# A router run once more on fewer tiles, logits in four column tiles, and loads on other queues and buffers

## The chip, the cores and the metric

The kernel runs on one core of one Trainium2 chip. The metric is the device time of one execution in microseconds (us), lower is better; several runs are made and the median counts. One further execution was recorded by the hardware profiler, and every row below is from that one. The engines are TensorE (PE, with its weight loads PEld), VectorE (DVE), ScalarE (ACT), GpSimd (POOL) and SyncE (SP), which here only issues DMAs. "L319" is line 319 of the kernel; the changed kernel's lines lie a few higher.

## The reference, cut to what matters

Three layers one behind the other, on 4 batches of 576 tokens of width 512 (8 heads of 64):

```python
def _attn_ref(q, k, v, phi):
    a = softmax of phi over the tokens
    k_m = np.einsum('bhsm,bhsd->bhmd', a, k)
    v_m = np.einsum('bhsm,bhsd->bhmd', a, v)
    scores = scale * np.matmul(q, k_m.transpose(0, 1, 3, 2))
    attn = softmax of scores over the 32 memories
    return np.matmul(attn, v_m).astype(np.float32)

def _moe_ref(x, w_in, w_out):
    h = x @ w_in
    g = h * (1.0 / (1.0 + np.exp(-h)))
    return (g @ w_out).astype(np.float32)

def _moe2_ref(x, w_gate, w_noise, noise, w1, w2):
    logits = x @ w_gate
    noise_scale = np.log1p(np.exp(x @ w_noise))
    noisy_logits = logits + noise_scale * noise
    top2 = np.argpartition(-noisy_logits, 2, axis=1)[:, :2]
    ...
    for e in range(E):
        for k in range(2):
            mask = top2[:, k] == e
            ...
            h = np.maximum(x[mask] @ w1[e], 0.0)
            out[mask] += top2_w[mask, k, None] * (h @ w2[e])
```

w_in (512 x 2048) and w_out (2048 x 512) arrive as float64; the 8 experts have w1 of 512 x 1024 and w2 of 1024 x 512.

## The kernel before, in words

**Attention and MLP.** The 2304 tokens are 18 tiles of 128: four whole ones in each batch, and a fifth that two batches share. Tiles 0 to 8 are those of batches 0 and 1, 9 to 12 of batch 2, 13 to 17 of batch 3 and the second shared one. The attention of a batch is folded into the first MLP matrix: `project` multiplies `w_in` by the batch's memories (L146), so that TensorE then goes from attention weights to the hidden layer (`mlp_h`, L258) and on to the output (`accumulate`, L280 to L282). Every operand is split into a high and a low part and takes three matmuls. ScalarE evacuates the hidden layer from PSUM with a tanh (L261), VectorE finishes the SiLU (L263), both make the two parts (L266, L267).

**Weights at the start.** `stage` brings a float64 block as pairs of 32-bit words into one of four buffers (tag `st`); `narrow` turns it into float32: ScalarE scales the upper word (L197), takes its sign (L198) and the lower word (L200, tile `lw`, one buffer), VectorE merges (L201), GpSimd multiplies by the sign (L202). There are 32 such steps. `w_in`, once narrowed, is also stored in DRAM (L220) and fetched again for each later batch into `wi`, two buffers (L214).

**The router.** When a tile of the MLP is done, `tile_a` copies it out (`xs`, L298) and stores it, `tile_b` transposes it (L312, L314: `xt`), `tile_c` computes 16 logits a token with four matmuls that accumulate in PSUM (L319), ScalarE copies them to `lz` (L320). `gate(j0, j1)` then works on tiles j0 to j1: some 30 small VectorE operations, a matmul for each token's rank in its expert (L396, L397), the slot (L414), and for each tile two indirect scatters of GpSimd into the table `tab_d` (L418). All scatters of a gate stand one behind the other in GpSimd's queue. Gates cover tiles 0 to 8, 9 to 12, 13 to 16 and 17.

**The experts.** `table(0)` loads the first expert's first rows of the table (L507, on SP's queue) and clips the index (L508); `gather(0)` fetches those tokens (L515), `flip` transposes them (L534). `fetch_w1(0, c)` and `split_w1(0, c)` load and split the first expert's w1 in four parts (L475; L483 on ScalarE, L484 on VectorE), in the `st` buffers. The experts follow in the tail (L551, L566, L571), writing to the output by scatter-add (L574).

**What sets the order.** The MLP runs in steps `s`, 32 for each batch (`SB`), its second half three steps (`LAG`) behind the first. Other work is hung on a step by `at(s, function, ...)`; the gates are called between two steps. The Tile framework then orders each engine's queue by priorities and adds the semaphores. Each engine runs its queue in that order, so one waiting instruction holds what stands behind it. PSUM has two `aux` and two `h` buffers for all short-lived products.

Of the kernel before, what the change touches and what calls it, by code (L numbers as in the profile page):

```python
# [20 lines left out]
NF = FF // 128  # L21
# [21 lines left out]
def body(ctx, tc, a):  # L43
# [21 lines left out]
    wgn = const.tile([128, 4, 16], F32, name="wgn")  # L65
# [127 lines left out]
    def narrow(t, m):  # L193
        top = t[:, :, 1].bitcast(F32)
        g = ap_.tile([128, 512], BF16, name="cg", bufs=2)
        mi = m.bitcast(I32)
        act.activation(m, top, AF.Copy, scale=2.0 ** -112)  # L197
        act.activation(g, top, AF.Sign)  # L198
        low = ap_.tile([128, 512], I32, name="lw", bufs=1)
        act.activation(low, t[:, :, 0].bitcast(U32), AF.Identity, scale=LOW, bias=lowb)  # L200
# [8 lines left out]
    def fetch_win(i):  # L209
        if i < NP:  # L210
            ST["i", i] = [stage(win[:, 2 * g:2 * g + 2, 2 * i * PW:2 * (i + 1) * PW]) for g in range(2)]
        else:
            WI[i] = m1.tile([128, 4, PW], F32, name="wi", bufs=2)
            sp.dma_start(WI[i].rearrange("p r f -> p (r f)"), win_d[i % NP])  # L214

    def narrow_win(i):
        WI[i] = m1.tile([128, 4, PW], F32, name="wi", bufs=2)
# [76 lines left out]
    XS, XT = {}, {}  # L294
# [21 lines left out]
    def tile_c(j):  # L316
        p = psum("aux", 2)
        for d in range(4):
            pe.matmul(p[:, :16], XT[j][:, d, :], wgn[:, d, :], start=(d == 0), stop=(d == 3))  # L319
        act.activation(lz[:, j, :], p[:, :16], AF.Copy)  # L320
# [7 lines left out]
    def routing_setup():  # L328
# [7 lines left out]
        for b in range(1, B, 2):  # L336
            j = TILES.index((b, 4))
            for x in range(2):
                pool.iota(tok[x * 64:(x + 1) * 64, j:j + 1], pattern=[[0, 1]], base=(b + x) * S - 64,
                          channel_multiplier=1, allow_small_or_imprecise_dtypes=True)  # L340
        sp.dma_start(wgn[:, :, 0:8], a["moe2_w_gate"].rearrange("(c p) e -> p c e", p=128))
# [129 lines left out]
    def fetch_w1(e, c):  # L471
        W1S[e, c] = P2["b"].tile([128, FE], F32, name="w1s", bufs=2) if e else \
            m1.tile([128, FE], F32, name="w1s", tag="st", bufs=4)
# [27 lines left out]
    def table(k):  # L501
# [5 lines left out]
        sp.dma_start(TAB[k].rearrange("p j w -> p (j w)"), t.rearrange("(p j) w -> p (j w)", j=n))  # L507
# [177 lines left out]
    ready = phi_max(0, 1)  # L685
    memory(0, 0)
    memory(0, 1)
    memory_t(0)
# [5 lines left out]
    with tc.issue_after(ready.ins):  # L694
        narrow_win(0)
# [47 lines left out]
    for b in range(B - 1):  # L743
# [10 lines left out]
        for k in range(1, n):  # L754
            at(s + k, tile_c, j + k)
            if k + 1 < n:
                at(s + k, tile_b, j + k + 1)
    s = 3 * SB
    at(s, open_a)
    at(s + 2, clear)  # L760
    for j in range(EARLY):
        at(s + 24 + 2 * j, flip, 0, j)
    for c in range(4):
        at(s + 4 + 4 * c, fetch_w1, 0, c)
        at(s + 10 + 4 * c, split_w1, 0, c)
# [13 lines left out]
    while s < total + LAG + 6:  # L779
# [4 lines left out]
        if s in (2 * SB, 4 * SB):  # L784
# [12 lines left out]
            else:  # L797
# [4 lines left out]
                for i, j in enumerate(range(13, 17)):  # L802
                    mlp_rest(b, range(cut[i], cut[i + 1]))
                    if j < 16:
                        tile_b(j + 1)
                    tile_c(j)
                gate(13, 17)
                mlp_rest(b, range(8, NF))
                for fn in (tile_a, tile_b, tile_c):
# [3 lines left out]
        if s == 2 * SB + LAG + 8:  # L813
            gate(0, 9)
# [44 lines left out]
```

## Time and profile before

| | us |
|---|---|
| median of 3 runs | 912.18 (911.67 to 913.01) |
| the profiled execution, its own time | 918.92 |
| its span in the trace | 917.1 |
| TensorE busy | 856.0 (93%) |
| VectorE busy | 462.0 (50%) |
| ScalarE busy | 366.3 (40%) |
| GpSimd busy | 252.2 (27%) |

The span is what the rows' times count from; 1.8 us of the execution lie around it. "Idle before" in a row is how long the engine stood still ahead of that instruction, and the name behind the arrow is what ended it ("issue": nothing that the profile shows; "remote": a semaphore whose setter it did not find). The granted clock is TensorE's, as a share of full speed.

### The profile page before, as it was taken

The page shows a single profiled execution, that of the slowest core. Times are in us where ns is not written, and L with a number is a line of the kernel's source. Part 1 is how long each engine was busy: PE and PEld are TensorE (multiplying, and loading weights), DVE is VectorE, ACT ScalarE, POOL GpSimd, SP SyncE. Part 2 cuts the span into 40 slices and gives each one's busy share as a digit, 9 for nine tenths or more (in the row PEclk, how much of TensorE's full clock was granted, in tenths as well). Part 3 has the DMA queues.
Part 4 walks back from the last instruction along what each step waited for, and adds up shares of the span by engine and source line. Part 5 has one row for each costly group of instructions (what it writes and reads, how often), then busy time and mean ns, then how long its engine had stood idle before and what let it go on. Part 6 is the DMA issues. An engine that isn't in the chain of part 4 may idle for free.

```text
span 917.1 us, 14389 instructions
## 1 busy us (share of the span) xinstructions
PE 856.0 (93%) x5504; PEld 724.5 (79%) x5504; DVE 462.0 (50%) x1070; ACT 366.3 (40%) x850; POOL 252.2 (27%) x279
## 2 busy tenths in 40 slices
PE   4698999999997899989999999999999999999995
PEld 2366678888885688868879998989989798897983
DVE  3787985575282755644553534344343444443410
ACT  3689974444232454443222532233323233231300
POOL 2555550000007000310342414234252352422311
PEclk9999999999999899999999999999999999999998
DMA  9798942532201118121243834364343644434311
GB/s 304 221 356 266 303 163 92 164 127 72 78 1 47 47 70 322 47 81 47 81 123 107 272 92 141 119 189 126 126 124 129 183 133 145 124 98 145 84 27 38
DMA packets 76166, 124.14 MB, mean 135 GB/s; under 512 B 27827, under 2 KB 39475, under 8 KB 76087
## 3 DMA queue, kind: packets, MB, share of 16 engines
q1 hardware_dynamic: 46343, 90.66, 30.0%
q0 software_dynamic: 29744, 32.46, 12.5%
q8 instruction: 45, 0.74, 0.3%
q14 instruction: 34, 0.28, 0.1%
HBM read 99.69 MB, written 23.81 MB: 135 GB/s over the span
## 4 chain that ended last, share of the span: by engine, by line
PE 71%; DVE 8%; ACT 6%; DMA 5%; issue 4%; POOL 3%; another core or an unknown queue 1%; SPq 1%; POOLq 0%; ACTq 0%; DVEq 0%
PE x L566 22%; PE x L551 11%; PE h L551 11%; PE h L258 7%; PE x L280 5%; PE x L282 4%; PE x L281 4%; PE aux L146 2%; PE aux L319 2%; PE aux L534 2%; DMA w1s<-moe_w 2%; POOL wo L202 1%; DMA kv<-kv 1%; DVE gl L267 1%
## 5 line engine op out<-in xcount | busy, mean ns | idle before, releaser
L566 PE MATMUL x<-w,gh 128*128 128x512 f32 (+5 forms) x640 | 202.4, 397 | 0.1
L566 PEld LDWEIGHTS x<-w,gh 128*128 128x128 f32 (+5 forms) x640 | 114.3, 183 | 28.0 <-ACT gh L553 0.5
L566 PE MATMUL x<-w,gl 128*128 128x512 f32 (+5 forms) x320 | 125.9, 393 | 0.2 <-DVE gl L554 0.2
L258 PE MATMUL h<-ah,wph 128*128 128x256 f32 (+1 forms) x512 | 113.3, 305 | 12.6 <-DVE th L263 4.8
L551 PE MATMUL h<-xh,w 128*128 128x290 f32 (+7 forms) x512 | 118.9, 303 | 0.0
L551 PE MATMUL x<-xh,w 128*128 128x290 f32 (+7 forms) x512 | 118.4, 303 | 0.0
L258 PEld LDWEIGHTS h<-ah,wph 128*128 128x128 f32 x512 | 90.6, 193 | 29.3 <-DVE th L263 8.1
L280 PE MATMUL x<-woh,gh 128*128 128x512 f32 x256 | 106.1, 417 | 4.5 <-ACT gh L266 2.2
L281 PE MATMUL x<-wol,gh 128*128 128x512 f32 x256 | 103.1, 403 | 6.4 <-issue 2.9
L282 PE MATMUL x<-woh,gl 128*128 128x512 f32 x256 | 102.0, 399 | 1.5 <-issue 1.0
L418 POOL DMA_INDIRECT tab_d<-rows,slot x36 | 35.4, 984 | 233.2 <-DVE slot L414 221.7
L263 DVE SCALAR_TENSOR_TENSOR th<-th,h 128x256 f32<-128x256 f32 (+1 forms) x128 | 57.7, 450 | 69.5 <-ACT th L261 53.5
L261 ACT ACTIVATE th<-h 128x256 f32<-128x256 f32 (+1 forms) x128 | 52.1, 407 | 90.7 <-PE h L258 72.0
L551 PEld LDWEIGHTS h<-xh,w 128*128 128x128 f32 x512 | 87.4, 189 | 0.3
L551 PEld LDWEIGHTS x<-xh,w 128*128 128x128 f32 x512 | 87.3, 188 | 0.0
L515 POOL DMA_INDIRECT xg<-x_d,gid x37 | 46.4, 1255 | 146.2 <-issue 76.9
L571 DVE SCALAR_TENSOR_TENSOR y<-x,tab,ex 116x512 f32<-116x512 f32 (+5 forms) x35 | 26.3, 750 | 108.0 <-PE x L566 103.6
L551 PE MATMUL x<-xl,w 128*128 128x290 f32 (+7 forms) x256 | 77.6, 303 | 0.5 <-DVE xl L538 0.5
L551 PE MATMUL h<-xl,w 128*128 128x290 f32 (+7 forms) x256 | 77.6, 303 | 0.0
L258 PE MATMUL h<-ah,wpl 128*128 128x320 f32 (+1 forms) x256 | 77.2, 302 | 0.3 <-DVE wpl L234 0.3
L574 POOL DMA_INDIRECT out<-y,tab x40 | 51.7, 1292 | 89.9 <-DVE y L571 82.8
L266 ACT ACTIVATE gh<-th 128x256 fp32r<-128x256 f32 x128 | 53.2, 416 | 52.9 <-DVE th L263 50.4
(158 smaller groups left out, 1421.7 us busy)
## 6 DMA issues: line engine op xcount, KB each, us to landing
w1s<-moe_w SPq DMA_DIRECT2D x32, 512.0 KB
w2s<-moe_w SPq DMA_DIRECT2D x32, 512.0 KB
wi<-win_d SPq DMA_DIRECT2D x24, 512.0 KB
kv<-kv SPq DMA_DIRECT2D x16, 650.0 KB
st<-moe_w_in SPq DMA_DIRECT2D x16, 512.0 KB
st<-moe_w_out SPq DMA_DIRECT2D x16, 512.0 KB
q<-qt SPq DMA_DIRECT2D x16, 288.0 KB
out<-z SPq DMA_DIRECT2D x1, 4608.0 KB
```

The source lines that it names most:

```text
L258: pe.matmul(p[:, :w], wt[:, g, c:c + 128], AH[b, g][at][:, t0:t0 + w], start=(n == 0), stop=(n == 5))
L261: act.activation(th[:, :w], p[:, :w], AF.Tanh, scale=0.5)
L263: dve.scalar_tensor_tensor(u[:, :w], th[:, :w], 1.0, p[:, :w], op0=OP.add, op1=OP.mult)
L266: act.activation(gh, u[:, :256], AF.Copy)
L280: pe.matmul(X2[j], gh[:, r], woh[f], start=(f == 0), stop=False)
L281: pe.matmul(X2[j], gh[:, r], wol[f], start=False, stop=False)
L282: pe.matmul(X2[j], gl[:, r], woh[f], start=False, stop=(f == NF - 1))
L418: st = pool.indirect_dma_start(out=tab_d, out_offset=bass.IndirectOffsetOnAxis(ap=slot[:, j, k:k + 1], axis=0), in_=rows.bitcast(I32)[:, j ...
L515: pool.indirect_dma_start(out=XG[k, j], out_offset=None, in_=x2_d if k else x2_d[:KNOWN, :], in_offset=bass.IndirectOffsetOnAxis(ap=GID[k] ...
L551: pe.matmul(p[:, :w], wt[:, d, c], x[:, d, r], start=(n == 0), stop=(n == 11))
L566: mm = pe.matmul(p, g[:, r], w[:, f, :], start=(n == 0), stop=(n == 23))
L574: st = pool.indirect_dma_start(out=a["out"], out_offset=bass.IndirectOffsetOnAxis(ap=TAB[k][:, j, 0:1], axis=0), in_=y, in_offset=None, bo ...
```

## The change

1. `gate(0, 9)` becomes `gate(0, 4)`, a batch earlier, and `gate(4, 9)` in the old place.
2. `tile_c` takes the padded gate weights `wgn` (four blocks of 128 x 32) as the stationary operand and the transposed tile as the moving one, so that the four matmuls write four blocks of 32 PSUM partitions. ScalarE copies 128 x 128 to `lt` (tag `st`). A new `tile_d`, a step later, transposes that on TensorE and adds the four blocks on VectorE.
3. `table(0)` is issued on GpSimd's queue.
4. Parts 2 and 3 of the first expert's w1 use the `wi` buffers, fetched at steps 20 and 21 and split at 24 and 27 of the last batch (before: 12 and 16, 18 and 22, in `st`); the flips go one step later.
5. `narrow_win(0)` is written ahead of batch 0's softmax, without its condition; `narrow` does the lower word first.

```diff
-    wgn = const.tile([128, 4, 16], F32, name="wgn")
+    wgn = const.tile([128, 4, 32], F32, name="wgn")
...
         mi = m.bitcast(I32)
+        low = ap_.tile([128, 512], I32, name="lw", bufs=1)
+        act.activation(low, t[:, :, 0].bitcast(U32), AF.Identity, scale=LOW, bias=lowb)
         act.activation(m, top, AF.Copy, scale=2.0 ** -112)
         act.activation(g, top, AF.Sign)
-        low = ap_.tile([128, 512], I32, name="lw", bufs=1)
-        act.activation(low, t[:, :, 0].bitcast(U32), AF.Identity, scale=LOW, bias=lowb)
...
         for d in range(4):
-            pe.matmul(p[:, :16], XT[j][:, d, :], wgn[:, d, :], start=(d == 0), stop=(d == 3))
-        act.activation(lz[:, j, :], p[:, :16], AF.Copy)
+            pe.matmul(p[d * 32:(d + 1) * 32, :128], wgn[:, d, :], XT[j][:, d, :], start=True, stop=True)
+        LT[j] = m1.tile([128, 128], F32, name="lt", tag="st", bufs=4)
+        act.activation(LT[j], p[:, :128], AF.Copy)
+
+    def tile_d(j):
+        p = spare(j)
+        pe.transpose(p[:, :128], LT.pop(j), ident)
+        dve.tensor_reduce(lz[:, j, :], p[:, :128].rearrange("p (d e) -> p e d", d=4)[:, :16, :], axis=AX.X, op=OP.add)
...
+        pool.memset(wgn, 0.0)
...
-            m1.tile([128, FE], F32, name="w1s", tag="st", bufs=4)
+            m1.tile([128, FE], F32, name="w1s", tag="st", bufs=4) if c < 2 else \
+            m1.tile([128, FE], F32, name="w1s", tag="wi", bufs=2)
...
-        sp.dma_start(TAB[k].rearrange("p j w -> p (j w)"), t.rearrange("(p j) w -> p (j w)", j=n))
+        (sp if k else pool).dma_start(TAB[k].rearrange("p j w -> p (j w)"), t.rearrange("(p j) w -> p (j w)", j=n))
...
     memory(0, 1)
+    narrow_win(0)
     memory_t(0)
...
-    with tc.issue_after(ready.ins):
-        narrow_win(0)
...
         for k in range(1, n):
+            at(s + k, tile_d, j + k - 1)
             at(s + k, tile_c, j + k)
...
-        at(s + 24 + 2 * j, flip, 0, j)
-    for c in range(4):
-        at(s + 4 + 4 * c, fetch_w1, 0, c)
-        at(s + 10 + 4 * c, split_w1, 0, c)
+        at(s + 25 + 2 * j, flip, 0, j)
+    for c, (x, y) in enumerate(((4, 10), (8, 14), (20, 24), (21, 27))):
+        at(s + x, fetch_w1, 0, c)
+        at(s + y, split_w1, 0, c)
...
+                mlp_rest(b, range(8, 10))
+                tile_d(16)
                 gate(13, 17)
-                mlp_rest(b, range(8, NF))
-                for fn in (tile_a, tile_b, tile_c):
+                mlp_rest(b, range(10, NF))
+                for fn in (tile_a, tile_b, tile_c, tile_d):
                     fn(17)
...
-        if s == 2 * SB + LAG + 8:
-            gate(0, 9)
+        if s == SB + LAG + 8:
+            gate(0, 4)
+        elif s == 2 * SB + LAG + 8:
+            gate(4, 9)
```

SP's queue around the first expert's weights `w1s`, before. `wi<-win_d` brings back narrowed weights, `x_d<-xs` stores finished tiles, `tab` is the table.

```order
L475 DMA w1s<-moe_w 128x1024
L214 DMA wi<-win_d 128x1024 x2
L475 DMA w1s<-moe_w 128x1024
L214 DMA wi<-win_d 128x1024 x2
L507 DMA tab_4275<-tab_d 128x6
L475 DMA w1s<-moe_w 128x1024 x2
L301 DMA x_d<-xs 128x512 x4
```

The same place in the changed kernel, and GpSimd's queue behind the scatters of gate(9,13) there.

```order
L483 DMA w1s<-moe_w 128x1024
L214 DMA wi<-win_d 128x1024 x2
L483 DMA w1s<-moe_w 128x1024
L214 DMA wi<-win_d 128x1024 x2
L483 DMA w1s<-moe_w 128x1024 x2
L301 DMA x_d<-xs 128x512 x4
```

```order
L363 MEMSET z 128x512
L425 DMA tab_d<-rows,slot 20480x2 x8
L515 DMA tab_4378<-tab_d 128x6
L516 TENSOR_SCALAR gid_4379<-tab_4378 128x3
L523 DMA xa<-x_d,gid_4379 128x512 x3
```

The table's load has left SP, where it stood ahead of the last two w1s, and stands on GpSimd between the scatters and the index step, where nothing stood.

ScalarE's first instructions, before and changed. `kvt` is batch 0's memories, `src` what it is made from; in the changed kernel the lower word is L198, the scaled upper word L199, the sign L200.

```order
L131 ACTIVATE src<-aux,rs 128x2x64
L197 ACTIVATE wi<-st 128x512
L131 ACTIVATE src<-aux,rs 128x2x64
L198 ACTIVATE cg<-st 128x512
L140 ACTIVATE kvt<-aux 128x256
L200 ACTIVATE lw<-st,lowb 128x512
L197 ACTIVATE wi<-st 128x512
L198 ACTIVATE cg<-st 128x512
L200 ACTIVATE lw<-st,lowb 128x512
L197 ACTIVATE wo<-st 128x512
```

```order
L131 ACTIVATE src<-aux,rs 128x2x64
L198 ACTIVATE lw<-st,lowb 128x512
L131 ACTIVATE src<-aux,rs 128x2x64
L199 ACTIVATE wi<-st 128x512
L200 ACTIVATE cg<-st 128x512
L199 ACTIVATE wi<-st 128x512
L198 ACTIVATE lw<-st,lowb 128x512
L200 ACTIVATE cg<-st 128x512
L140 ACTIVATE kvt<-aux 128x256
L198 ACTIVATE lw<-st,lowb 128x512
L199 ACTIVATE wo<-st 128x512
```

The evacuation of `kvt` stands behind five instructions of narrow steps instead of two, and `lw` ahead of its step's other two.

TensorE where batch 0's second tile gets its logits, before and changed.

```order
L280 MATMUL x_1752<-woh_90,gh 128x512
L281 MATMUL x_1752<-wol_106,gh 128x512
L282 MATMUL x_1752<-woh_90,gl 128x512
L258 MATMUL h<-ah_1408,wph 128x320
L319 MATMUL aux<-wgn,xt 128x16 x4
L258 MATMUL h<-ah_1409,wph 128x320
L258 MATMUL h<-ah_1408,wpl 128x320
L312 MATMUL aux<-ident,xs 128x128 x4
L258 MATMUL h<-ah_1488,wph 128x320
L258 MATMUL h<-ah_1489,wph 128x320
L258 MATMUL h<-ah_1488,wpl 128x320
L280 MATMUL x_1788<-woh_90,gh 128x512
```

```order
L258 MATMUL h<-ah_1409,wph 128x320
L325 MATMUL aux<-ident,lt 128x128
L258 MATMUL h<-ah_1410,wph 128x320
L258 MATMUL h<-ah_1409,wpl 128x320
L258 MATMUL h<-ah_1489,wph 128x320
L258 MATMUL h<-ah_1490,wph 128x320
L319 MATMUL aux<-xt,wgn 32x128 x4
L312 MATMUL aux<-ident,xs 128x128 x4
L258 MATMUL h<-ah_1489,wpl 128x320
L325 MATMUL aux<-ident,lt 128x128
L280 MATMUL x_1790<-woh_90,gh 128x512
L281 MATMUL x_1790<-wol_106,gh 128x512
```

The logits' four matmuls have 128 columns in place of 16, with operands exchanged, and a transpose of `lt` follows some instructions later for each tile.

## Rows read from the trace of the kernel before

**Rows 1.** Page, part 1: busy us, share and instructions of each engine, whole span.

```profile
PE 856.0 (93%) x5504; PEld 724.5 (79%) x5504; DVE 462.0 (50%) x1070; ACT 366.3 (40%) x850; POOL 252.2 (27%) x279
```

**Rows 2.** Windows: length, busy us (PE, PEld, DVE, ACT, POOL), granted clock, DMA share, GB/s.

```profile
60.00:120.00 60.00, 51.98 (x392) 36.94 (x392) 50.36 (x95) 54.07 (x120) 32.69 (x30) 1.00 0.86 287
283.50:303.00 19.50, 9.75 (x63) 6.36 (x63) 2.38 (x7) 1.80 (x5) 12.55 (x13) 0.80 0.02 1
303.00:306.00 3.00, 3.00 (x13) 2.64 (x12) 2.96 (x6) 0.62 (x2) 0.00 (x0) 0.61 0.00 0
344.00:361.50 17.50, 17.50 (x137) 14.85 (x136) 7.83 (x18) 6.56 (x20) 0.00 (x0) 1.00 0.98 352
377.30:387.20 9.90, 9.90 (x58) 8.78 (x57) 3.96 (x10) 3.38 (x10) 7.72 (x8) 1.00 0.34 108
396.50:408.00 11.50, 7.32 (x31) 5.62 (x31) 7.21 (x16) 5.87 (x16) 2.37 (x3) 0.85 0.36 116
```

**Rows 3.** Timeline of TensorE: start, us, line, names, count, idle before and its end.

```profile
288.93 1.10 PE L146 MATMUL aux<-q,kvt 64*32 64x320 f32 x16 [2.50 <-issue]
```

**Rows 4.** Timeline of GpSimd: scatters of gate(0,9), first, last; of gate(9,13), first.

```profile
276.82 1.13 POOL L418 DMA_INDIRECT tab_d<-rows,slot  x1 [138.76 <-DVE slot L414]
...
298.80 0.96 POOL L418 DMA_INDIRECT tab_d<-rows,slot  x1 [0.30 <-issue]
...
377.29 0.97 POOL L418 DMA_INDIRECT tab_d<-rows,slot  x1 [33.55 <-DVE slot L414]
```

**Rows 5.** Timeline of ScalarE: first MLP evacuation at the end of each.

```profile
299.16 0.39 ACT L261 ACTIVATE th<-h 128x256 f32<-128x256 f32 x1 [13.97 <-remote]
...
387.38 0.44 ACT L261 ACTIVATE th<-h 128x320 f32<-128x320 f32 x1 [3.05 <-PE h L258]
```

**Rows 6.** Timeline of SP's DMA queue: table and w1s.

```profile
391.73 0.33 SPq L507 DMA_DIRECT2D tab<-tab_d  x1
392.23 6.12 SPq L475 DMA_DIRECT2D w1s<-moe_w  x2
```

**Rows 7.** Timeline of ScalarE: splits of w1s.

```profile
396.04 1.15 ACT L483 ACTIVATE w<-w1s 128x512 fp32r<-128x512 f32 x2 [4.38 <-DMA w1s<-moe_w]
...
402.72 1.15 ACT L483 ACTIVATE w<-w1s 128x512 fp32r<-128x512 f32 x2 [2.63 <-DMA w1s<-moe_w]
```

**Rows 8.** Timeline of TensorE, 396 to 409 us: two gaps, the first flip.

```profile
398.39 0.51 PE L258 MATMUL h<-ah,wph 128*128 128x256 f32 x2 [1.86 <-DVE th L263]
...
404.23 0.70 PE L280 MATMUL x<-woh,gh 128*128 128x512 f32 x1 [2.04 <-ACT gh L266]
...
408.03 0.60 PE L534 MATMUL aux<-ident,xa 128*128 128x128 f32 x4
```

**Rows 9.** Timeline of TensorE: a tile's logits, the matmul behind, the nearest forms.

```profile
260.01 0.38 PE L112 MATMUL aux<-ident,mt 128*128 128x128 f32 x2
...
260.23 0.96 PE L319 MATMUL aux<-wgn,xt 128*128 128x16 f32 x8
...
261.04 0.48 PE L280 MATMUL x<-woh,gh 128*128 128x512 f32 x1
...
264.88 2.42 PE L124 MATMUL aux<-kv,phi 128*32 128x130 f32 x80
```

**Rows 10.** Groups by form: busy us, mean ns; the logits' copy, the nearest reduce.

```profile
L320 ACT ACTIVATE lz<-aux 128x16 f32<-128x16 f32 x18 | 3.3, 184 | 22.4 <-PE aux L319 22.4
...
L110 DVE TENSOR_REDUCE mt<-aux 128x1 f32<-128x128 f32 x8 | 2.3, 289 | 2.6 <-PE aux L108 2.6
```

**Rows 11.** Timeline of TensorE: gate(0,9)'s rank matmul.

```profile
272.02 0.21 PE L396 MATMUL aux<-g,tri 128*128 128x72 bf16 x1 [0.89 <-DVE g L393]
```

**Rows 12.** Timeline of GpSimd: the table's index step.

```profile
394.85 0.25 POOL L508 TENSOR_SCALAR gid<-tab 128x3 int32<-128x3 int32 x1 [7.70 <-DMA tab<-tab_d]
```

**Rows 13.** Groups by form: the narrow steps' Sign and merge.

```profile
L198 ACT ACTIVATE cg<-st 128x512 bf16<-128x512 f32 x32 | 21.2, 661 | 0.0
...
L201 DVE SCALAR_TENSOR_TENSOR wi<-wi,lw 128x512 int32<-128x512 int32 x16 | 12.8, 801 | 8.0 <-ACT lw L200 7.8
```

More of the change, by code (lines that the diff above doesn't have):

```diff
@@ L212, in fetch_win @@
         else:
-            WI[i] = m1.tile([128, 4, PW], F32, name="wi", bufs=2)
+            WI[i] = m1.tile([128, 4, PW], F32, name="wi", tag="wi", bufs=2)
             sp.dma_start(WI[i].rearrange("p r f -> p (r f)"), win_d[i % NP])
     def narrow_win(i):
-        WI[i] = m1.tile([128, 4, PW], F32, name="wi", bufs=2)
+        WI[i] = m1.tile([128, 4, PW], F32, name="wi", tag="wi", bufs=2)
         for g, t in enumerate(ST.pop(("i", i))):
@@ L292, in mlp_rest @@
             accumulate(TILES.index((b, 4)), gh, gl, slice(0, 128), f)
-    XS, XT = {}, {}
+    XS, XT, LT = {}, {}, {}
     def tile_a(j):
@@ L684, in body @@
     phi_max(0, 0)
-    ready = phi_max(0, 1)
+    phi_max(0, 1)
     memory(0, 0)
     memory(0, 1)
+    narrow_win(0)
     memory_t(0)
@@ L757, in body @@
                 at(s + k, tile_b, j + k + 1)
+        at(s + n, tile_d, j + n - 1)
     s = 3 * SB
@@ L805, in body @@
                         tile_b(j + 1)
+                    if j > 13:
+                        tile_d(j - 1)
                     tile_c(j)
+                mlp_rest(b, range(8, 10))
+                tile_d(16)
                 gate(13, 17)
-                mlp_rest(b, range(8, NF))
-                for fn in (tile_a, tile_b, tile_c):
+                mlp_rest(b, range(10, NF))
+                for fn in (tile_a, tile_b, tile_c, tile_d):
                     fn(17)
```

## The prediction

> **What bounds the kernel now.** I read the busy shares first. TensorE is busy 93% of the span and every other engine half or less [rows 1], so the time is TensorE's own work plus the 61 us (917.1 − 856.0) in which it stands still. So I went to the busy time by stretch, to find where it stands or is granted a low clock. Outside the first 120 us, whose load of weights keeps the DMA queues about 0.9 and ScalarE 90% busy [rows 2], two places stand out that the change touches.
>
> *First place, 283.5 to 306 us.* TensorE is busy for 9.75 of 19.5 us at a granted clock of 0.80, then for three full us at 0.61, a mix of its two levels (1.2 and 2.4 GHz) [rows 2]. So 9.75 us are lost by standing, 9.75 × 0.20 = 1.95 and 3 × 0.39 = 1.2 by the clock: 12.9 us. TensorE's first gap ends at 288.93 after 2.50 us, so it begins at 286.4, and it waits there for nothing that the profile shows [rows 3]. What runs meanwhile is GpSimd's row of 18 scatters of gate(0,9), L418, from 276.82 to 299.76, 1.27 us from one to the next [rows 4]. ScalarE's next evacuation of an MLP tile starts at 299.16 after 13.97 us of idleness, put down to a remote releaser, and again after 3.05 us at 387.38 [rows 5], where the 8 scatters of gate(9,13) run (377.29, 8 × 1.27 us: to 387.3) and TensorE loses nothing: 9.90 busy of 9.90 [rows 2, 4]. I read this as: what TensorE finishes stops reaching its readers some way into a run of scatters, and does so until the run ends. ScalarE's idleness begins at 299.16 − 13.97 = 285.2 and at 387.38 − 3.05 = 384.3, 8.4 and 7.0 us after the first scatter; TensorE, which is ahead of it, stops 286.4 − 276.8 = 9.6 us after the first scatter in the first case and not at all in the second, where the run ends after 10.2 us. So a run costs TensorE what it has over 9.6 us: 22.9 − 9.6 = 13.3 for the 18, near the 12.9 counted.
>
> *Second place, 396.5 to 408 us.* TensorE is busy for 7.32 of 11.5 us at 0.85 [rows 2]: 4.18 standing and 1.1 of clock, 5.3 us. Its gaps of 1.86 and 2.04 us end with VectorE's and ScalarE's steps of the MLP [rows 8]; ScalarE was itself in front of the split of the first expert's weights (L483), 4.38 and 2.63 us for the DMA w1s [rows 7]. These two loads were issued behind the table's load, which sits on SP's queue at 391.73 because it waits for the last scatters [rows 6].
>
> **The change part by part**, against the profiled execution's 918.92 us (917.1 of span and 1.8 around it; 6.7 above the median of 912.18).
>
> *Gate in four and five tiles.* Two runs of 8 and 10 scatters take the place of the 18. By the 9.6 us above, a run of 8 (10.2 us) loses 0 to 0.6, and as 377 us shows none I take 0.3. A run of 10 (12.7 us) loses 12.7 − 9.6 = 3.1. So 12.9 − 3.4 = **−9.5**. The bounds are 0 (the blocked time stays as a total) and −12.9. The second gate's some 30 small VectorE steps lie where VectorE is half idle; what TensorE sees of a gate is the wait ahead of its rank matmul, 0.89 us at 272.02 [rows 11]: one more such wait, bounds 0 and 0.9, **+0.5**.
>
> *Table on GpSimd's queue, w1s in the other buffers.* Weights 2 and 3 are then fetched at steps 20 and 21 behind nothing of the scatters and split at 24 and 27, which is where the flips of the gathered rows now run, 408.03 [rows 8], about 12 us behind the old wait. Their buffers come free with the last projection, some way ahead of that. **−5.3**; bounds 0 (another wait of that size) and −5.3. On GpSimd the table's load delays only what follows it there, its index step L508, which waits 7.70 us for that load now and starts at 394.85 [rows 12]; the gathers behind it feed the flips 13 us later. So 0; if that cover went, the table's delay would be paid once, about 1 us. The Trainium skill ("DMA: Bandwidth & Descriptors", Specifications) speaks against this move: first bytes come after about 1 us on GpSimd's path and 0.6 on SP's. By it the table lands some 0.4 us later, an estimate, which those 13 us hide; no run here has the same load on both.
>
> *Logits.* A tile's four matmuls (8 instructions, L319) hold TensorE from 260.23 to 261.04, 0.81 us [rows 9]. The new form has no row. The nearest for four column tiles with a stationary of 32 columns is L124, 80 instructions with 130 moving columns in 2.42 us, 0.03 each: 8 × 0.03 = 0.24; the nearest for the transpose is L112 at 260.01, 2 in 0.22 us [rows 9]. Together 0.46, or 0.35 saved; the lower bound is 0 (each matmul as slow as now), the upper 0.5. 13 tiles lie where TensorE is the bound: 13 × 0.35 = **−4.6**. The five of the tail save the same, but the tail is a chain through ScalarE, VectorE and the gathers, and tile_d adds a step to it: **−1**, bounds −2 and +1. Off TensorE, the evacuation of 128x16 in 184 ns becomes one of 128x128 and a reduce like L110's of 289 ns [rows 10], about 0.35 us more a tile and 6.4 in all, on engines 40 and 50% busy [rows 1]: hidden. The Trainium skill ("TensorEngine Tiling (Array Packing)", PSUM Bottleneck) says that tiling speeds up TensorE "but not PSUM evacuation", and that the copy may become the bound. By that rule the −4.6 would go. No run here shows it yet; the shares of the two engines speak against it, and its case is rival 3.
>
> *New waits.* The logits' copy lt takes one of the four buffers that xs and xt use, and in tile 11 that buffer was last the source z of the zeroing of out, a transfer that fills the DMA engines to 361.5 [rows 2]. ScalarE issues in order, so the MLP's evacuations queue behind it: bounds 0 and 2.5 us, less TensorE's lead: **+0.8**.
>
> *Startup.* narrow_win(0) comes earlier, and in each of 32 narrow steps the low half goes first. Its result has one buffer: before, two ScalarE steps lay between it and the next use; now the Sign of 0.66 us covers VectorE's merge of 0.80 [rows 13], so 0.1 to 0.2 us of each may show, 3 to 6 us on ScalarE; against it, the chain to GpSimd's product is shorter by one such step (0.66), and staging buffers come free earlier. The copy of kvt, on batch 0's chain, stands behind three more narrow instructions, some 2 us once. Taken as **0**, bounds −4 and +4, as the DMA queues, not ScalarE alone, set the pace there [rows 2].
>
> The sum: −9.5 + 0.5 − 5.3 − 4.6 − 1 + 0.8 = **−19.1**: 899.8 for the profiled execution. The runs shown lie 6.7 below it: 893.1 if the losses are as long in them, near 900 if the 6.7 is part of the losses that go. I say **895**.
>
> **Rivals.**
> 1. *The blocking goes by scatters, not by the length of a run.* For it: nothing shows why the results stop. Against it: 8 scatters at 377 cost TensorE nothing. Then the 18 still cost 12.9: −19.1 + 9.5 = −9.6, so about **903**.
> 2. *Slower: the single buffer of the low half binds the startup.* ScalarE is 54.07 of 60 us busy there [rows 2]. If VectorE is late by its whole merge each time, 32 × 0.70 to 0.80 = 22 to 26 us are added to the stage that all later work waits for; above 19.1 us, some 0.6 us for each narrow step, the change loses. Net +3 to +7: **915 to 919**. For it, too: VectorE is busy for 50.36 of the 60 us, so a merge may come late. Against it: a merge that comes at once has the Sign as cover for 0.66 of its 0.80 us, and the DMA share of 0.86 says that ScalarE often waits for weights anyway.
> 3. *The evacuation binds*: the two aux buffers of PSUM that tile_c and tile_d share with the projections come free only after ScalarE's copy and VectorE's reduce, and TensorE waits for them by the 6.4 us that these grow. −19.1 + 6.4 = −12.7, from the median 899.5, with the 2 us that my figure stands over 893.1: **about 901**. Against it: the shares of rows 1. The rule of the Trainium skill quoted above (PSUM Bottleneck) is this case.
>
> **How the numbers follow.** My forecast has 0.68, rival 1 0.14, rival 3 0.12, rival 2 0.06. The forecast's own ends: 893.1 with 4 of startup, and the rest of the 3.4 of scatters gone, is 886; 900 is its upper end. To hold 8 in 10 the range takes in rivals 1 and 3 with a few us of startup: **886 to 906**. A change of under 0.2% (1.8 us) can't be told from none. Below 910.4 lie all but rival 2 and a little of the others: faster 0.93, same 0.02, slower 0.05.
>
> **What would show it.** No TensorE gap above 1 us during 8 scatters, and some 3 us during the 10; no wait of L483 on w1s near 396 us; four logits' matmuls and one transpose in 0.46 us a tile; GpSimd's index step within 2 us of its old place; TensorE's idle time from 60 to 120 us (60 − 51.98 = 8.0) unchanged within 4. A gap of over 8 us near the gates would prove the first reading wrong, a later end of the narrow steps the startup's, and idle time put down to lt or its reduce the logits'.

## The result, and the profile after

The changed kernel's median is 900.81 us (900.09 to 903.92, 4 runs), the kernel before's 911.92 (910.25 to 913.01, 4 runs). The ratio is 0.9886, interval 0.9858 to 0.9914: about 10.4 us faster. The interval is one of 95%, and so are all below. The profiled executions are further apart, 918.92 and 900.53, which is 18.4 us: the profiled execution of the kernel before lies above all four of its timed ones. The forecast was 895 (886 to 906), faster.

The changed kernel's page, part 1, to be read against [rows 1]:

```profile
PE 846.7 (94%) x5524; PEld 712.3 (79%) x5524; DVE 467.1 (52%) x1117; ACT 368.0 (41%) x852; POOL 253.7 (28%) x281
```

TensorE has 9.3 us less to do by this count and stands still for 52.0 us (898.7 − 846.7) in place of 61.1. The windows of the places of [rows 2] (length, busy us and instructions of PE, PEld, DVE, ACT and POOL, granted clock, DMA share, GB/s): the second half of the startup, the run of 8 scatters, the run of 10, and the place where the last weights are split:

```profile
60.00:120.00 60.00, 51.51 (x394) 39.25 (x395) 47.29 (x94) 54.30 (x119) 31.15 (x29) 0.97 0.79 270
173.20:183.50 10.30, 10.30 (x96) 8.14 (x96) 5.13 (x12) 4.99 (x14) 7.87 (x8) 1.00 0.89 155
274.00:286.70 12.70, 12.70 (x112) 9.53 (x90) 7.22 (x18) 5.39 (x14) 9.68 (x10) 1.00 0.37 85
371.00:387.00 16.00, 16.00 (x112) 13.08 (x111) 9.18 (x22) 8.51 (x22) 4.53 (x6) 1.00 0.34 82
```

In this execution the new runs of scatters and the wait for w1s cost TensorE nothing: 10.30 of 10.30, 12.70 of 12.70 and 16.00 of 16.00 us, at full clock. From 60 to 120 us TensorE stands for 8.5 us (8.0 before). GpSimd's timeline of the changed kernel (start, us, line, names, idle before and what ended it), with the first and last scatter of gate(4,9), the table's load and its index step:

```profile
273.95 0.96 POOL L425 DMA_INDIRECT tab_d<-rows,slot  x1 [90.75 <-DVE slot L421]
...
285.46 0.97 POOL L425 DMA_INDIRECT tab_d<-rows,slot  x1 [0.30 <-issue]
...
377.15 0.58 POOL L515 DMA_DIRECT2D tab<-tab_d  x1 [5.01 <-DMA tab_d<-rows,slot]
382.87 0.47 POOL L516 TENSOR_SCALAR gid<-tab 128x3 int32<-128x3 int32 x1 [5.13 <-DMA tab<-tab_d]
```

ScalarE's timeline of the same kernel, with the first of the two late splits of w1s:

```profile
381.28 1.16 ACT L491 ACTIVATE w<-w1s 128x512 fp32r<-128x512 f32 x2 [1.79 <-DMA w1s<-moe_w]
```

The ten scatters run without a break like the 18 of [rows 4]. L491 is the old L483 of [rows 7]: 1.79 us of waiting for w1s in place of 4.38 and 2.63. Of TensorE's waits (us in total, times, longest) three bear on the change:

```profile
PE aux L542 <- DMA xg<-x_d,gid: 5.7, 2, 3.4
...
PE aux L403 <- DVE g L400: 2.6, 4, 0.8
...
PE aux L319 <- DVE lz L326: 0.4, 2, 0.2
```

L542 is the tail's flip, which waited 1.6 us for its gathered rows before; L403 is the old L396 of [rows 11], whose four waits came to 2.5 us; L319 waits for the reduce that frees its PSUM buffer. The one wait of L403 that is new is that of gate(0,4), here on TensorE's timeline:

```profile
170.46 0.19 PE L403 MATMUL aux<-g,tri 128*128 128x32 bf16 x1 [0.80 <-DVE g L400]
```

Where the 18.4 us of the two profiled executions come from is best read from the starts of the same MLP evacuation (L261 on ScalarE's timeline, counted from 0) in both traces:

| up to | before | after | difference | gained in this piece |
|---|---|---|---|---|
| evacuation 28, startup over | 130.05 | 128.12 | −1.9 | −1.9 |
| 64, batch 1's tiles, gate(0,4) in the changed one | 225.52 | 224.54 | −1.0 | +0.9 |
| 78, batch 2's tiles done | 281.37 | 279.47 | −1.9 | −0.9 |
| 88, behind the scatters | 319.72 | 304.20 | −15.5 | −13.6 |
| 112, batch 3's tiles done | 383.03 | 366.82 | −16.2 | −0.7 |
| 124, behind the split of w1s | 417.89 | 395.40 | −22.5 | −6.3 |
| the end | 917.1 | 898.7 | −18.4 | +4.1 |

In this pair the tail gives 4.1 us back. Of the pieces, the one at the scatters is the largest, and it is also the one that the medians (10.4 us) don't show in full.

### The profile page after: what moved, and what is told of

Read it like the earlier page. It is cut to its first block, busy times and chain, and to the rows that moved or that the text cites. A ratio compares the mean times of both kernels' runs of the same rounds, so it can differ in the third digit from the quotient of the medians.

```text
span 898.7 us, 14532 instructions
## 1 busy us (share of the span) xinstructions
PE 846.7 (94%) x5524; PEld 712.3 (79%) x5524; DVE 467.1 (52%) x1117; ACT 368.0 (41%) x852; POOL 253.7 (28%) x281
## 4 chain that ended last, share of the span: by engine, by line
PE 79%; DVE 7%; ACT 5%; DMA 4%; POOL 2%; issue 1%; SPq 1%; POOLq 0%; DVEq 0%; ACTq 0%
PE x L574 24%; PE x L559 12%; PE h L559 11%; PE h L258 8%; PE x L280 6%; PE x L282 6%; PE x L281 6%; PE aux L146 2%; PE aux L542 2%; DMA st<-moe_w_out 1%; ACT lw L198 1%; DMA kv<-kv 1%; DVE gl L267 1%; POOL wo L202 1%; PE aux L319 1%
## 5 line engine op out<-in xcount | busy, mean ns | idle before, releaser
L258 PE MATMUL h<-ah,wph 128*128 128x320 f32 (+1 forms) x512 | 110.7, 302 | 5.6 <-DVE th L263 2.4
L280 PE MATMUL x<-woh,gh 128*128 128x512 f32 x256 | 106.6, 418 | 2.3 <-ACT gh L266 1.8
L258 PEld LDWEIGHTS h<-ah,wph 128*128 128x128 f32 x512 | 90.2, 191 | 21.3 <-DVE th L263 4.4
L282 PE MATMUL x<-woh,gl 128*128 128x512 f32 x256 | 102.1, 399 | 0.7 <-POOL gl L267 0.5
L261 ACT ACTIVATE th<-h 128x256 f32<-128x256 f32 (+1 forms) x128 | 52.0, 407 | 72.5 <-PE h L258 72.1
L258 PE MATMUL h<-ah,wpl 128*128 128x320 f32 (+1 forms) x256 | 76.6, 300 | 0.0
```

Source lines behind the costliest of these rows:

```text
L258: pe.matmul(p[:, :w], wt[:, g, c:c + 128], AH[b, g][at][:, t0:t0 + w], start=(n == 0), stop=(n == 5))
L261: act.activation(th[:, :w], p[:, :w], AF.Tanh, scale=0.5)
L280: pe.matmul(X2[j], gh[:, r], woh[f], start=(f == 0), stop=False)
L282: pe.matmul(X2[j], gl[:, r], woh[f], start=False, stop=(f == NF - 1))
```

## The experiments

Three sets of four kernels. The kernels of one set ran on one chip, each set on another, and the kernel before is timed in each: 907.64 us (35 runs) in the first, 907.29 (20) in the second, 919.75 (13) in the third. So each kernel is judged by its ratio to the kernel before in its own set.

**First set: is the gap at the scatters a matter of the run's length?**

The kernel before, unchanged, for a second trace.

> The kernel before, once more, for a second profile. Theory (a long run of scatters holds back what TensorE finishes): the gap near gate(0,9) is there again, but, as the runs lie 6.7 us under the first profiled execution, some 6 us long and not 13; time 912. Rival (the stall was an accident of one execution): no TensorE gap over 1 us between 280 and 306 us; time 912.

907.86 us, ratio 1.0001 (0.9983 to 1.0020). GpSimd's timeline of this execution, first and last scatter of gate(0,9):

```profile
277.22 1.14 POOL L418 DMA_INDIRECT tab_d<-rows,slot  x1 [138.76 <-DVE slot L414]
...
300.53 0.97 POOL L418 DMA_INDIRECT tab_d<-rows,slot  x1 [0.30 <-issue]
```

A window over most of them (columns as above):

```profile
286.00:301.50 15.50, 15.50 (x124) 12.60 (x123) 13.55 (x26) 7.23 (x17) 12.15 (x12) 1.00 0.26 14
```

The same 18 scatters, one behind the other as in [rows 4], and TensorE is busy for 15.50 of 15.50 us where [rows 2] had 9.75 of 19.50. The rival's sign is there: no gap.

The gates alone:

```diff
-        if s == 2 * SB + LAG + 8:
-            gate(0, 9)
+        if s == SB + LAG + 8:
+            gate(0, 4)
+        elif s == 2 * SB + LAG + 8:
+            gate(4, 9)
```

> The kernel before with gate(0,4) and gate(4,9) in place of gate(0,9), nothing else. Theory (length of the run of scatters): 5 to 7 us faster, 905 to 907, no TensorE gap over 1 us near either gate. Rival (accident of one execution, the change's gain is in its other parts): 912, within 1.

907.44 us, ratio 1.0001 (0.9984 to 1.0018): nothing gained. One gate, the slots and scatters in two parts (LAST is the latest VectorE step of the MLP at that point):

```diff
-        done = dve.scalar_tensor_tensor(slot[:, j0:j1, :], xf, float(NS), r2, op0=OP.mult, op1=OP.add)
+        if j0 == 0:
+            done = dve.scalar_tensor_tensor(slot[:, :4, :], xf[:, :4], float(NS), r2[:, :4], op0=OP.mult, op1=OP.add)
+            scatter(0, 4)
+            def later():
+                with tc.issue_after(LAST[0].ins):
+                    dve.scalar_tensor_tensor(slot[:, 4:9, :], xf[:, 4:], float(NS), r2[:, 4:], op0=OP.mult, op1=OP.add)
+                    scatter(4, 9)
...
+        elif s == 2 * SB + LAG + 22:
+            rest.pop()()
```

> The kernel before with its one gate(0,9), whose last step (the slots) is made in two: four tiles at once, five tiles some 26 us later, so the 18 scatters go in runs of 8 and 10. Theory (length of the run): as the split gates alone, 905 to 907. Rival (it is the gate's own operations that count, or nothing does): 912, within 1.

907.09 us, ratio 0.9993 (0.9979 to 1.0008). And two gates with one run:

```diff
+        if (j0, j1) == (0, 4):
+            done = dve.scalar_tensor_tensor(slot0, xf, float(NS), r2, op0=OP.mult, op1=OP.add)
+            return done
...
+        if j0 == 4:
+            with tc.issue_after(done.ins):
+                dve.tensor_copy(slot[:, :4, :], slot0)
+        for j in range(0 if j0 == 4 else j0, j1):
```

> The kernel before with gates on four and five tiles at their two steps, but the first one's slots held back in a copy until the second's, so that all 18 scatters go in one run again. Theory (length of the run): the gain is gone, 912 to 913. Rival (the split of the gate's operations gains): as the split gates alone, below 910.

907.57 us, ratio 0.9998 (0.9982 to 1.0015). The window of its 18 scatters from the seventh on:

```profile
282.00:298.20 16.20, 16.20 (x139) 12.66 (x138) 12.98 (x26) 6.78 (x18) 12.79 (x12) 1.00 0.29 22
```

No gap here either. On this chip nothing that was done to the gates or their scatters moved the time by more than its interval, because there was no gap to remove. By this set the gap looks like an accident of one execution; the third set's traces show that it isn't (below).

**Second set: which part of the change gains?** The changed kernel, and the changed kernel with one part undone at a time.

> The changed kernel once more, beside the kernels below on one chip. The one long gap that the gates were to remove was no part of the kernel's time (the split gates alone gained nothing), so what is left is the weights' wait (5.3), the startup (2) and the logits (about 2), less what the tail gives back (2 to 4): 6 to 9 us under the kernel before. If the first pair of results was of another kind, 11.

900.58 us, ratio 0.9923 (0.9895 to 0.9951): 7.0 us faster here, within the first expectation. The loads undone:

```diff
-        (sp if k else pool).dma_start(TAB[k].rearrange("p j w -> p (j w)"), t.rearrange("(p j) w -> p (j w)", j=n))
+        sp.dma_start(TAB[k].rearrange("p j w -> p (j w)"), t.rearrange("(p j) w -> p (j w)", j=n))
...
-            m1.tile([128, FE], F32, name="w1s", tag="st", bufs=4) if c < 2 else \
-            m1.tile([128, FE], F32, name="w1s", tag="wi", bufs=2)
+            m1.tile([128, FE], F32, name="w1s", tag="st", bufs=4)
...
-        at(s + 25 + 2 * j, flip, 0, j)
-    for c, (x, y) in enumerate(((4, 10), (8, 14), (20, 24), (21, 27))):
-        at(s + x, fetch_w1, 0, c)
-        at(s + y, split_w1, 0, c)
+        at(s + 24 + 2 * j, flip, 0, j)
+    for c in range(4):
+        at(s + 4 + 4 * c, fetch_w1, 0, c)
+        at(s + 10 + 4 * c, split_w1, 0, c)
```

> The changed kernel with the table's load on SP again, w1s all in the st buffers at the old steps and the flips at theirs. Theory (the wait of ScalarE for w1s behind the table): 3 to 5 us slower than the changed kernel, with L483's wait back near 380 us; all 5.3 if the tail gives nothing back. Rival (the tail waits for the last tiles' table anyway, so the wait was hidden): within 1.

905.82 us, ratio 0.9987 (0.9968 to 1.0007): 0.0064 × 907.3 = 5.8 us of the 7.0 go with the loads. ScalarE's timeline of this kernel, its two splits:

```profile
380.15 1.15 ACT L490 ACTIVATE w<-w1s 128x512 fp32r<-128x512 f32 x2 [3.94 <-DMA w1s<-moe_w]
...
387.55 1.15 ACT L490 ACTIVATE w<-w1s 128x512 fp32r<-128x512 f32 x2 [2.91 <-DMA w1s<-moe_w]
```

TensorE's timeline of it, the gap between them and the end of the second:

```profile
389.89 0.50 PE L258 MATMUL h<-ah,wph 128*128 128x256 f32 x2 [3.27 <-DVE th L263]
```

The two waits of [rows 7] are back (3.94 and 2.91 us), and with them a TensorE gap of 3.27 us. SP's queue has the two loads in the changed kernel, and in this one behind the table:

```profile
376.14 0.81 SPq L483 DMA_DIRECT2D w1s<-moe_w  x2
...
376.47 6.00 SPq L482 DMA_DIRECT2D w1s<-moe_w  x2
```

The first goes out at nearly the same time, the second 5.5 us later. The logits undone (tile_c as before, with wgn of 16 columns and no zeroing of it; tile_d empty):

```diff
-            pe.matmul(p[d * 32:(d + 1) * 32, :128], wgn[:, d, :], XT[j][:, d, :], start=True, stop=True)
-        LT[j] = m1.tile([128, 128], F32, name="lt", tag="st", bufs=4)
-        act.activation(LT[j], p[:, :128], AF.Copy)
+            pe.matmul(p[:, :16], XT[j][:, d, :], wgn[:, d, :], start=(d == 0), stop=(d == 3))
+        act.activation(lz[:, j, :], p[:, :16], AF.Copy)
```

> The changed kernel with the old logits (four accumulating matmuls with 16 columns, ScalarE's copy, no transpose, no reduce). My forecast's theory (0.35 us saved a tile, 13 tiles in the bound part): 4.6 us slower. Rival (the transpose also lengthens its neighbours, and the later lz makes the first gate's matmul wait): 1 to 3 us slower.

899.74 us, ratio 0.9912 (0.9882 to 0.9942): not slower. 4.6 us would be a ratio of 0.9974, outside the interval. So neither the forecast's term nor the rival's lower end of 1 us was found; by the two intervals an effect of up to some 3 us can't be excluded. Between the same two evacuations, number 30 and 126, the new form gains 1.2 us: 265.48 us against 266.66. That stretch with new logits (e5), as a window:

```profile
133.95:399.43 265.48, 262.96 (x1974) 214.64 (x1973) 166.39 (x497) 120.46 (x323) 31.23 (x33) 1.00 0.33 99
```

Its TensorE groups by line (count, then busy us, mean ns, idle before):

```profile
L319 PE MATMUL aux<-xt,wgn 128*32 128x128 f32 x104 | 6.3, 284 | 0.4 <-DVE lz L326 0.4
...
L325 PE MATMUL aux<-ident,lt 128*128 128x128 f32 x13 | 3.8, 289 | 0.0
```

The same stretch with old logits (e7), as a window:

```profile
135.49:402.15 266.66, 264.99 (x1961) 223.14 (x1960) 165.09 (x484) 120.47 (x323) 31.44 (x33) 1.00 0.33 99
```

And its group by line:

```profile
L319 PE MATMUL aux<-wgn,xt 128*128 128x16 f32 x104 | 13.1, 258 | 0.0
```

The matmuls themselves go from 13.1 to 6.3 us for 13 tiles, the transposes add 3.8, and TensorE's busy time falls by 2.03 (264.99 − 262.96) where the two lines alone would give 3.0. Its idle time rises by 0.85 (from 1.67 to 2.52). Net 1.2 where 4.6 was forecast. These busy times overlap, so it is clearer to count from the start of one instruction to the start of the next, as the forecast did. A tile's four matmuls, the instruction behind them, a transpose and the instruction behind it, on TensorE's timeline of e5:

```profile
260.87 0.42 PE L319 MATMUL aux<-xt,wgn 128*32 128x128 f32 x8
261.22 0.50 PE L281 MATMUL x<-wol,gh 128*128 128x512 f32 x1
...
261.80 0.27 PE L325 MATMUL aux<-ident,lt 128*128 128x128 f32 x1
261.82 0.54 PE L258 MATMUL h<-ah,wph 128*128 128x320 f32 x2
```

The new form holds TensorE for 0.35 and 0.02 us here, the old one for 0.81 [rows 9]. Over the 13 tiles of the stretch this way of counting gives 11.15 us with the old logits and 5.88 (5.29 and 0.59) with the new: 5.3 us less. The MLP's own matmuls (L258, L280 to L282), equal in number, take 2.9 us more in e5 than in e7, and that is most of what is lost between 5.3 and 2.03. Why they take longer is not shown. Then the tail, where GpSimd's timeline has the last scatter and the first index step, with new logits (e5):

```profile
438.41 1.43 POOL L425 DMA_INDIRECT tab_d<-rows,slot  x1 [0.31 <-issue]
449.71 0.23 POOL L516 TENSOR_SCALAR gid<-tab 128x2 int32<-128x2 int32 x1 [9.87 <-DMA tab<-tab_d]
```

and with old ones (e7):

```profile
445.24 2.09 POOL L421 DMA_INDIRECT tab_d<-rows,slot  x1 [0.30 <-issue]
454.57 0.23 POOL L512 TENSOR_SCALAR gid<-tab 128x2 int32<-128x2 int32 x1 [7.24 <-DMA tab<-tab_d]
```

The router is 6.8 us earlier with the new logits (438.41 against 445.24), but its table's index step only 4.9 us. TensorE's wait for the rows gathered behind it, from the waits of e5:

```profile
PE aux L542 <- DMA xg<-x_d,gid: 5.0, 2, 3.0
```

and from those of e7:

```profile
PE aux L538 <- DMA xg<-x_d,gid: 2.3, 1, 2.3
```

2.7 us more. So TensorE reaches the flip sooner and waits for the same chain of scatter, table and gather. All traces bear this out: this wait is 4.9 to 5.7 us in the four with the new logits, 0.9 to 4.1 in the ten with the old. The startup undone (narrow's old order, narrow_win(0) behind its condition):

```diff
-        low = ap_.tile([128, 512], I32, name="lw", bufs=1)
-        act.activation(low, t[:, :, 0].bitcast(U32), AF.Identity, scale=LOW, bias=lowb)
         act.activation(m, top, AF.Copy, scale=2.0 ** -112)
         act.activation(g, top, AF.Sign)
+        low = ap_.tile([128, 512], I32, name="lw", bufs=1)
+        act.activation(low, t[:, :, 0].bitcast(U32), AF.Identity, scale=LOW, bias=lowb)
...
-    narrow_win(0)
...
+    with tc.issue_after(ready.ins):
+        narrow_win(0)
```

> The changed kernel with narrow's old order and narrow_win(0) in its old place behind its condition. Theory (the startup as changed is 2 us shorter, as the milestones of the two traces show): 2 us slower. Rival (the 2 us are found again later or vary from execution to execution): within 1.

901.93 us, ratio 0.9933 (0.9912 to 0.9954): 0.9 us slower than the changed kernel, with intervals that overlap widely. That is the rival's sign, and unclear between the two at the end. At evacuation 28 the traces are clear: the nine with the old startup stand there at 129.66 to 130.60 us, the five with the new at 126.94 to 129.12, some 2 us earlier. A part is lost again at once: from evacuation 28 to 64 the nine take 95.5 to 95.8 us, the five 96.1 to 96.5. So the +0.9 of the table above goes with the new startup more than with the new gate: e12 below, which has one gate(0,9), takes 96.12, and e2, with the new gates and the old startup, 95.68. What takes the time is open.

**Third set: which half of the loads, and are they enough?** Each is the kernel before with parts of the change. First the table:

```diff
-        sp.dma_start(TAB[k].rearrange("p j w -> p (j w)"), t.rearrange("(p j) w -> p (j w)", j=n))
+        (sp if k else pool).dma_start(TAB[k].rearrange("p j w -> p (j w)"), t.rearrange("(p j) w -> p (j w)", j=n))
```

> The kernel before with only the table's load on GpSimd's queue. Theory (the last two w1s are late because SP's queue holds them behind the table, which waits for the scatters to land): ScalarE's two waits for w1s go, 4 to 5 us faster. Rival (they are late because their st buffers come free late, or because they are split too early): 0 to 2 us faster, L483 still waits near 383 us.

913.57 us, ratio 0.9920 (0.9895 to 0.9944): 7.4 us, more than the theory said. ScalarE's timeline of it, the last splits of w1s:

```profile
391.52 1.13 ACT L483 ACTIVATE w<-w1s 128x512 fp32r<-128x512 f32 x2
...
397.01 1.15 ACT L483 ACTIVATE w<-w1s 128x512 fp32r<-128x512 f32 x2 [1.39 <-DMA w1s<-moe_w]
```

and SP's queue with their loads:

```profile
377.40 16.42 SPq L475 DMA_DIRECT2D w1s<-moe_w  x2
```

One wait is gone, and the other is 1.39 us. The first load now goes out at 377.40, where it stood behind the table at 392.23 [rows 6]: the queue was the cause of that wait, as the theory had it. The second still goes out only at 393.5, when VectorE's half of the split before (L484, ends at 393.46) has freed its st buffer, which is the rival's reason. Then the weights, with the table left on SP:

```diff
-            m1.tile([128, FE], F32, name="w1s", tag="st", bufs=4)
+            m1.tile([128, FE], F32, name="w1s", tag="st", bufs=4) if c < 2 else \
+            m1.tile([128, FE], F32, name="w1s", tag="wi", bufs=2)
...
-        at(s + 24 + 2 * j, flip, 0, j)
-    for c in range(4):
-        at(s + 4 + 4 * c, fetch_w1, 0, c)
-        at(s + 10 + 4 * c, split_w1, 0, c)
+        at(s + 25 + 2 * j, flip, 0, j)
+    for c, (x, y) in enumerate(((4, 10), (8, 14), (20, 24), (21, 27))):
+        at(s + x, fetch_w1, 0, c)
+        at(s + y, split_w1, 0, c)
```

> The kernel before with only w1s parts 2 and 3 in the wi buffers, fetched at steps 20 and 21, split at 24 and 27, flips one step later; the table's load stays on SP ahead of them. Theory (the split 12 us later leaves time enough for the queue): 4 to 5.5 us faster. Rival (the queue behind the table binds still): 0 to 2 us faster.

915.10 us, ratio 0.9934 (0.9908 to 0.9959): 6.1 us. ScalarE's timeline, the first of the late splits:

```profile
396.55 1.16 ACT L484 ACTIVATE w<-w1s 128x512 fp32r<-128x512 f32 x2 [0.32 <-DMA w1s<-moe_w]
```

0.32 us: the later split is as good a cure, with the table still on SP. Both of these edits in one kernel:

> The kernel before with the table's and w1s' loads as changed, nothing else of the change. Theory (of the whole change only the loads gain in the end): 5 to 6 us faster, within 1.5 of the whole change's 7. Rival (logits and startup gain beside them and the loads alone give less): under 4 us faster.

915.07 us, ratio 0.9941 (0.9912 to 0.9970): 5.4 us. The two halves don't add up; each removes the same wait. The stretch from evacuation 112 to 124 says it more sharply than the medians: 34.86 us in the first trace of the kernel before and 34.31 in e1, 28.31 with the table alone, 28.30 with the weights alone, and 29.69 with both, 1.2 of which is a gap near the scatters (below). With the startup beside them (the edit of e8 the other way round):

> The kernel before with the loads and the startup as changed, old logits, one gate(0,9). Theory (startup 1 to 2 us, logits and gates nothing): 6.5 to 8 us faster, as good as the whole change or up to 1 us better. Rival (the logits are worth 2 to 5 us): 3 to 5 us faster, behind the whole change.

913.03 us, ratio 0.9905 (0.9877 to 0.9934): 8.7 us by its ratio, a little above the theory. That is as much as the whole change's 0.9923 in the second set, with intervals that overlap, so no version is shown to beat the changed kernel.

These four have the old gate(0,9), and on this chip the gap is there. GpSimd's timeline of e9, first and last scatter of gate(0,9), first of gate(9,13):

```profile
276.55 1.14 POOL L418 DMA_INDIRECT tab_d<-rows,slot  x1 [138.80 <-DVE slot L414]
...
298.54 0.97 POOL L418 DMA_INDIRECT tab_d<-rows,slot  x1 [0.30 <-issue]
...
377.22 0.97 POOL L418 DMA_INDIRECT tab_d<-rows,slot  x1 [33.55 <-DVE slot L414]
```

The windows of e9 around them:

```profile
283.00:302.00 19.00, 11.19 (x66) 6.31 (x65) 2.25 (x6) 1.80 (x5) 12.56 (x13) 0.87 0.03 2
302.00:306.00 4.00, 3.78 (x11) 3.18 (x12) 3.65 (x6) 1.05 (x4) 0.00 (x0) 0.50 0.00 0
382.00:392.50 10.50, 10.50 (x87) 8.73 (x85) 4.58 (x13) 4.76 (x14) 4.46 (x5) 1.00 0.03 5
```

ScalarE's timeline of e9, its evacuation at the end of the idle time:

```profile
295.94 0.39 ACT L261 ACTIVATE th<-h 128x256 f32<-128x256 f32 x1 [11.02 <-remote]
```

TensorE is busy for 11.19 of 19 us, then at a granted clock of 0.50, its lower level of 1.2 GHz, for 4 us. ScalarE's evacuation stood for 11.02 us. e10, e11 and e12 show the same (11.06, 10.29 and 11.78 us). So of seven traces with 18 scatters in one run, five have the gap (the kernel before's first and these four) and two (e1, e4) don't, and the two are of the chip on which the kernel before takes 907.6 us, the four of the one on which it takes 919.8. The size of the gap hardly varies: from evacuation 78 to 88 the five traces with it take 38.35 to 38.83 us, and all nine others, whatever their gates, 24.73 or 24.74.

In the same execution of e9 the run of 8 that starts at 377.22 costs TensorE nothing: 10.50 of 10.50 us. But a short run is not free on this chip. In e11 the run of 8 that starts at 378.34 holds ScalarE's evacuation back, and then TensorE, as their timelines have it:

```profile
389.91 0.44 ACT L261 ACTIVATE th<-h 128x320 f32<-128x320 f32 x1 [4.48 <-PE x L282]
...
390.92 0.56 PE L258 MATMUL h<-ah,wph 128*128 128x320 f32 x2 [1.20 <-DVE th L263]
```

At this run of 8 ScalarE's longest wait is 3.05 to 4.48 us in the five traces that have the gap, and 0.97 in the nine that haven't. So there the 8 scatters hold ScalarE back too, and mostly TensorE's lead covers it.

Left open: the split gates on a chip that shows the gap. Each set ran on one chip, and that the chip decides is read off from which sets show the gap; no run takes it away or brings it about on one chip, so this is not shown further. No kernel with runs of 8 and 10 in place of the 18 was traced on a chip that has it, as the kernels that would tell ran in the first set. That the changed kernel's traces have no gap (its first and e5) is therefore no proof for the split. The first pair's medians fit neither kind of chip clearly: 911.92 lies between the 907 and the 920 of the sets. So how much of the pair's 10.4 us is the gap stays open; the second set, without it, has 7.0.

## Why the prediction was right, and where its terms were not

The time lies in the range and the sign is right. The sum of −19.1 came within 1 us of the two profiled executions' −18.4, but the two agree in large part because both rest on the same execution of the kernel before, with its gap. The medians moved by 10 or 11, and in the second set, whose traces have no gap, by 7.0, of which the loads are 5.8. That the range held is in good part luck: the gates and the logits, 15.1 of the 19.1, can't be found in that 7.0.

- **The gates, −9.5.** The mis-sized term. The step that failed is "a run costs TensorE what it has over 9.6 us": e1 and e4 have runs of 18 scatters, over 24 us long, without loss. The gap goes with the chip in these traces: 13.6 to 14.1 us between evacuations 78 and 88 where it occurs, 0 where it doesn't, and one trace can't show that. The changed kernel's 10 scatters show none of the 3.1 us that the step gave them, but they were not traced where the gap is known to occur; on such a chip only e11's 1.20 us at a run of 8, where the step allows 0 to 0.6, speaks against it. The 6.7 us between the profiled execution and the median was the hint; I put my figure between the two cases, when it was the term itself that was in doubt. Rival 1 (it goes by scatters, not by the run) has e9 against it, where 8 in a row cost TensorE nothing and 18 do, and e11 a little for it, where 8 cost 1.20 us. The one more gate, +0.5: L403 waits 0.80 us at gate(0,4), within the bounds 0 and 0.9, but not for the gate's sake. The same wait is 0.79 or 0.80 us in all four traces with the new logits and 0.00 in the three with the old ones (e2, e4, e7), so it goes with the new logits.
- **The loads, −5.3.** Right: 5.8 by e5 and e6, 5.4 by e11. The working was right about the queue (e9), but not about the twelve us of distance. ScalarE comes to the split at 379.49 (381.28 − 1.79) where it came to it at 376.21 (380.15 − 3.94) in e6: 3.3 us later. That and the second load's earlier issue leave 1.79 us of the wait. And the two edits are not a sum; either does it.
- **The table on GpSimd's queue, 0.** Right in what it costs, not in the sign given for it (index step within 2 us of its old place: 382.87 is 4.2 behind 394.85 less the 16.2 us gained before). Its index step stood 5.72 us behind its issue (377.15 to 382.87), against 3.12 us on SP [rows 6, 12], and the flips hid it. The rule of the Trainium skill ("DMA: Bandwidth & Descriptors", Specifications), 1 us to the first byte in place of 0.6, doesn't account for the difference. With old logits (e7) the same load on the same queue takes 2.14 us to its index step, as GpSimd's timeline of that kernel has it:

```profile
377.70 0.59 POOL L511 DMA_DIRECT2D tab<-tab_d  x1 [4.51 <-DMA tab_d<-rows,slot]
379.84 0.25 POOL L512 TENSOR_SCALAR gid<-tab 128x3 int32<-128x3 int32 x1 [1.55 <-DMA tab<-tab_d]
```

The traces divide by the order of issue. Where the two w1s loads of 512 KB go out just ahead of the table's 3 KB (the changed kernel's two traces, e8, e12), it takes 5.35 to 5.72 us; where the table goes first or its neighbours have long gone (e7, e9, e11), 1.96 to 2.14.

- **The logits, −4.6 and −1.** Too large: 1.2 us in the MLP's stretch, nothing that the timing finds at the end. The prices of the instructions themselves held: 5.88 us for 13 tiles is 0.45 a tile, where 0.46 was forecast, and the old ones took 0.86. The step that failed is that TensorE saves what these instructions save, that is, that the MLP's matmuls beside them stay as long as they were: TensorE's busy time fell by 2.0 and not by 5.3, as those matmuls took 2.9 us more, and its waits grew by 0.85. The Trainium skill's rule ("TensorEngine Tiling (Array Packing)", PSUM Bottleneck) agrees with this trace in kind: TensorE waits for the evacuation, but only for the 0.4 us of L319 behind lz, far from the 6.4 of rival 3.
- **The tail, −1.** Wrong in sign in the profiled pair: 4.1 us were given back. One reason is shown: TensorE came to the flip of the gathered rows sooner than the chain of scatters, table and gather (5.7 us of waiting for xg, 1.6 before). The 4.1 itself is not: from evacuation 124 to the end the ten traces with the old logits take 498.8 to 507.1 us, the four with the new 501.7 to 503.3. I had named that chain and not asked what it does to the other gains.
- **lt behind the zeroing, +0.8.** Not found: in the changed kernel's trace TensorE stands for 0.02 us from 300 to 350 us, and batch 3's tiles gain 0.7 us, as in every trace with the new logits.
- **The startup, 0 within 4.** Within its bounds: some 2 us faster at evacuation 28 in all traces, of which about 0.7 is lost again by evacuation 64; at the end 0.9 by e5 and e8 and 3.3 by e11 and e12, neither of which the timing tells from 0. Rival 2 (the low half's single buffer binds) fell: 8.5 us of standing from 60 to 120 us, against 8.0.

## What to carry to other kernels

A gap for which the profile names no cause is not a term of a sum before a second trace of the same kernel shows it; that the profiled execution lies above the median is a reason to ask. Before two edits are added up, ask whether they remove the same wait, as the table's and the weights' loads did here. And ahead of a fixed chain (here scatter, table, gather) a gain is worth what the chain leaves of it: read the wait at its end first.

## What was not expected of the hardware

- The same program with the same 18 indirect scatters lost about 14 us on one chip and nothing on another, and the kernel before's medians differ by 12 us between these chips (919.75 and 907.64).
- In the gap the DMA engines are idle (a share of 0.02 to 0.03), TensorE still issues now and then, and ScalarE's next evacuation comes only after 10 to 14 us. In the first trace the matmuls that it reads had ended at 286.4 (L258, 286.14 and 0.28 long), and it began at 299.16. Why is open.
- Two edits to the DMA loads, the table's and the weights', freed the same stretch of some 6 us each, and both together no more.
- A 3 KB load took 1.96 to 2.14 us to the step that reads it, and 5.35 to 5.72 us when two loads of 512 KB had gone out on another queue up to 1 us before it.
